# Attention and a spectral mix in one kernel: v of unit 8 in 16 small loads on SyncE's queue

## Chip, core and metric

The kernel runs on one core of a Trainium2 chip. Its time is the device time of one execution in microseconds (us); where several executions are given, their median is the number that counts. Lower is better.

## What is computed

Two layers follow each other. The first is an attention with feature maps. q, k and v have the shape (8 batches, 8 heads, 576 tokens, 64 channels). The second takes the result as x with the shape (8, 576, 512), filters 64 frequencies of each sequence with complex weights of 512 by 512, and adds a channel product with a ReLU. Everything is in float32 at the interface.

```
def phi(x):
    proj = einsum('bhsd,df->bhsf', x, w_phi)
    proj = proj - max(abs(proj), axis=-1, keepdims=True)
    return concatenate([exp(proj), exp(-proj)], axis=-1)
q_p, k_p = phi(q), phi(k)
kv = einsum('bhsf,bhsd->bhfd', k_p, v);  z = sum(k_p, axis=2)
x  = einsum('bhsf,bhfd->bhsd', q_p, kv) / (einsum('bhsf,bhf->bhs', q_p, z)[..., None] + 1e-6)
# x is laid out as (8, 576, 512)
X = rfft(x, axis=1);  Y[:, :64] = X[:, :64] @ (w_r + i*w_i)   # one 512x512 matrix per mode
u = x + irfft(Y)
out = u + maximum(u @ w_ch, 0)
```

The two weight tensors hold 64 x 512 x 512 float32 each, 64 MiB each. They are far the largest part of what has to come from memory.

## The kernel before, in words

**Units.** The attention is cut into 16 units. A unit is two batches of two heads (class `Unit`, L101); unit number n has g = n // 4 (the pair of heads) and bp = n % 4 (the pair of batches). So unit 8 is (g, bp) = (2, 0). Each unit needs three loads: `load_k` and `load_q` (L105, L109), which turn float32 into bfloat16 on the way and are 288 KB each as they land, and `load_v` (L113), which stays float32 and is 576 KB. All three go through the helper `load` (L94), which makes one DMA over 128 partitions. The v tile `vn` has two buffers (pool `pin`, L85), so v of unit n goes into the buffer that unit n - 2 has used.

**The loop.** The loop at L503 works on several units at once, in a pipeline: at step n it finishes unit n - 1 (`P`), runs the middle of unit n (`Q`), starts unit n + 1 (`K`) and turns k and q of unit n + 2 (`R`). `weigh_v2` (L182) of unit n is the one reader of its v: two VectorE multiplications `va<-vn,ee`. Right after it, at L514, the loop asks for v of unit n + 2, on GpSimd's queue (POOL). v of units 0 and 1 is asked for ahead of the loop on SyncE's queue (SP, L368 and L371). After these and the two loads of w_phi, SP has nothing to do until it stores and copies in the second half of the kernel.

**The weights.** `wload` (L340) loads an eighth of the modes for one g and one of w_r and w_i: 1 MB as it lands in bfloat16, twice that as it is read. There are 64 of them. They land in nine rotating buffers (`pw`, L83) and in some places that are free at first (`home`, L327). `next_w` (L359) issues the next one; it is called after each `mix` (L461), which multiplies the frequencies of one g by one such load. All weights, all k, q and v of the loop, and w_ch are issued by POOL, one after the other, in the order of the program (`InOrder`, L26, keeps each engine's instructions in the order in which they are written down).

**The second half.** From L574 on the last weights come in while the products with w_ch and the inverse transform are worked off. The list of those is spread over the weight loads in the loop at L923, so that TensorE has work while it waits for a weight. The last weight's `mix` comes when this list is empty. After it, the last modes are added to the outputs, and SP stores these (`store`).

**Semaphores of DMAs.** The framework gives each DMA of POOL one of eight completion semaphores in turn (the trace's landing marks carry the numbers 99 to 106 for them), and each DMA of SP one of another eight. In the trace a POOL DMA goes out only after the one eight places ahead of it has landed: the weight load of 137.26 us goes out 0.5 us after that one's landing at 136.73.

Of the kernel before, what the change touches and what calls it, by code (L numbers as in the profile page):

```python
# [21 lines left out]
NP = 4  # L22
MG = 8
NO = NMODES // MG


class InOrder:
# [16 lines left out]
def kernel(  # L44
# [15 lines left out]
    pool, sp = InOrder(tc, nc.gpsimd), InOrder(tc, nc.sync)  # L60
# [17 lines left out]
    xs = xflat[:, 16:].rearrange("p (g b n d) -> p g b n d", g=NG, b=NP, n=18)  # L78
    yacc = pers.tile([128, NO, DMODEL], F32, name="yacc")

# [13 lines left out]
    def load(t, src, g, bp, eng):  # L94
        eng.dma_start(
            t.rearrange("p b c d -> p b (c d)"),
            src[2 * bp:2 * bp + 2, 2 * g:2 * g + 2].rearrange("b h (p c) d -> (h p) b (c d)", c=9),
        )


    class Unit:  # L101
# [10 lines left out]

        def load_v(self, eng=pool):  # L113
            self.vn = pin.tile([128, 2, 9, D_], F32, name="vn")
            load(self.vn, v, self.g, self.bp, eng)

        def turn(self, src, dst, flat, part):

# [231 lines left out]
    wts = {}  # L350
    wq = [(g, mg) for g in range(2) for mg in range(2 * NO)]
    wq += [(g, mg) for g in (2, 3) for mg in range(12)]
# [29 lines left out]
    mi = scr[:, 2048:2112].bitcast(I32)  # L382
    pool.iota(mi, [[4, 2], [8, NO], [1, 4]], base=0, channel_multiplier=0)
    ident_f = scr[:, 2176:2304]
# [538 lines left out]
    while mixq:  # L923
        key = mixq.pop(0)
        g, o, i = key[0], key[1] // 2, key[1] % 2
# [128 lines left out]
```

## Time and profile before

| what | value |
|---|---|
| median of 9 runs | 440.91 us (440.36 to 442.49) |
| the profiled execution's own time | 440.36 us |
| its span, first to last instruction | 438.6 us |
| what lies outside the span | 1.8 us |
| PE busy / VectorE / ScalarE / POOL | 75% / 68% / 64% / 26% of the span |
| DMA | 99.55 MB as landed, 163.64 MB read from HBM |
| POOL's v loads (14) | 576 KB each, 24.7 us from issue to landing (median) |
| SP's v loads (units 0 and 1) | 576 KB each, 6.6 us |
| weight loads on POOL | 1024 KB each, 28.4 and 28.6 us |

A page of the profile shows one execution. `va<-vn,ee` names an instruction by the tile that it writes and those that it reads. Nearly all instructions are recorded at L37, since a helper there passes them on; so groups are told apart by tile names. "DMA wt<-in_moe_w_i_dram" is a load of weights, "vn<-in_v_dram" one of v. In a timeline the first number is the start, the second the duration, and the brackets at the end tell how long the engine had been idle before and what ended that. Beside the instructions, the trace holds a record of each DMA packet (start, duration, bytes, queue) and a mark of each DMA engine's landing: 16 marks for each DMA, one from each of the core's 16 DMA engines. The records don't tell which of the 16 engines a packet ran on.

### The profile page before, as it was taken

The page shows a single profiled execution, that of the slowest core. Times are in us where ns is not written, and L with a number is a line of the kernel's source. Part 1 is how long each engine was busy: PE and PEld are TensorE (multiplying, and loading weights), DVE is VectorE, ACT ScalarE, POOL GpSimd, SP SyncE. Part 2 cuts the span into 40 slices and gives each one's busy share as a digit, 9 for nine tenths or more (in the row PEclk, how much of TensorE's full clock was granted, in tenths as well). Part 3 has the DMA queues.
Part 4 walks back from the last instruction along what each step waited for, and adds up shares of the span by engine and source line. Part 5 has one row for each costly group of instructions (what it writes and reads, how often), then busy time and mean ns, then how long its engine had stood idle before and what let it go on. Part 6 is the DMA issues. An engine that isn't in the chain of part 4 may idle for free.

```text
span 438.6 us, 10106 instructions
## 1 busy us (share of the span) xinstructions
PE 329.3 (75%) x4190; PEld 201.0 (46%) x4233; DVE 296.0 (68%) x583; ACT 279.2 (64%) x478; POOL 112.5 (26%) x151
## 2 busy tenths in 40 slices
PE   1687677578678787787885777374679998998993
PEld 1355456456456455464554555251335454333320
DVE  5667876877785777866778878342883333885684
ACT  2786876887897676865778877310644442765782
POOL 6232132132211223222222131121101121582072
PEclk9998786999998689886889998885999999999997
DMA  8999999999999999999999999999999999997787
GB/s 192 211 210 211 234 216 237 229 220 240 236 212 238 216 232 237 237 211 238 222 226 237 211 239 212 239 212 212 212 215 223 220 221 223 212 219 155 239 364 309
DMA packets 51710, 99.55 MB, mean 227 GB/s; under 512 B 2512, under 2 KB 13648, under 8 KB 51664
## 3 DMA queue, kind: packets, MB, share of 16 engines
q0 software_dynamic: 45232, 85.86, 99.7%
q1 hardware_dynamic: 6432, 13.04, 8.6%
q8 instruction: 33, 0.54, 0.4%
q14 instruction: 13, 0.11, 0.1%
HBM read 163.64 MB, written 9.44 MB: 395 GB/s over the span
## 4 chain that ended last, share of the span: by engine, by line
DMA 34%; PE 31%; DVE 16%; ACT 12%; issue 5%; POOL 1%; POOLq 0%; ACTq 0%; DVEq 0%
PE pt L37 13%; DMA vn<-in_v_dram 11%; PE one L37 10%; DMA wt<-in_moe_w_r_dram 8%; DMA wt<-in_moe_w_i_dram 8%; ACT AB L37 6%; PE two L37 6%; DMA kb<-in_k_dram 5%; DVE mk L37 4%; DVE m L37 3%; ACT AQ L37 2%; DMA qb<-in_q_dram 2%; PE pp L37 2%; ACT XT L37 1%; DVE xw L37 1%
## 5 line engine op out<-in xcount | busy, mean ns | idle before, releaser
L37 ACT ACTIVATE AB<-two 128x1024 bf16<-128x1024 f32 x64 | 62.0, 1026 | 12.6 <-DVE mk L37 9.2
L37 ACT ACTIVATE AQ<-two 128x1024 bf16<-128x1024 f32 x64 | 62.6, 1044 | 1.8 <-PE two L37 1.5
L37 ACT CAST xw<-pt 128x512 bf16<-128x512 f32 x50 | 29.3, 587 | 41.8 <-PE pt L37 41.6
L37 DVE TENSOR_REDUCE m<-two 128x8 f32<-128x1024 f32 x32 | 39.2, 1224 | 14.1 <-PE two L37 14.0
L37 DVE TENSOR_TENSOR va<-vn,ee 128x1152 bf16<-128x1152 f32 x32 | 42.0, 1355 | 9.5 <-DMA vn<-in_v_dram 9.5
L37 DVE TENSOR_REDUCE mk<-two 128x8 f32<-128x1024 f32 x32 | 38.9, 1218 | 9.4 <-PE two L37 9.4
L37 POOL DMA_DIRECT2D wt<-in_moe_w_i_dram x28 | 20.9, 748 | 86.7 <-PE pt L37 40.4
L37 POOL DMA_DIRECT2D wt<-in_moe_w_r_dram x30 | 22.5, 750 | 70.2 <-PE one L37 31.0
L37 PE MATMUL pt<-wchb,xT 128*128 128x512 bf16 x127 | 34.3, 382 | 6.1 <-DVE xT L37 4.6
L37 ACT COPY qT<-one 128x512 bf16<-128x512 bf16 (+1 forms) x32 | 19.4, 641 | 29.9 <-PE one L37 29.5
L37 PEld LDWEIGHTS <-xs 128*128 128x128 bf16 x624 | 31.3, 102 | 13.2 <-issue 8.0
L37 PE MATMUL two<-w2blk,qT 128*128 128x256 bf16 x128 | 22.1, 301 | 19.3 <-ACT AB L37 8.3
L37 PE MATMUL one<-wt,XT 128*32 128x512 bf16 x304 | 27.1, 446 | 5.9 <-DMA wt<-in_moe_w_i_dram 4.4
L37 PEld LDWEIGHTS <-qT 128*128 128x128 bf16 x144 | 14.7, 105 | 36.8 <-issue 33.3
L37 PE MATMUL two<-mT,minus 96*128 96x512 bf16 x64 | 28.3, 443 | 3.5 <-issue 1.9
L37 PEld LDWEIGHTS <-AQ 128*128 128x128 bf16 x512 | 25.8, 111 | 8.5 <-issue 5.2
L37 PE MATMUL one<-va,AB 64*128 64x65 bf16 x1024 | 22.7, 200 | 8.9 <-DVE va L37 8.9
L37 PE MATMUL one<-kvz,AQ 128*128 128x65 bf16 x512 | 28.5, 213 | 0.8 <-ACT qT L37 0.8
L37 DVE COPY xT<-pt 128x512 bf16<-128x512 bf16 x36 | 17.0, 472 | 16.8 <-PE pt L37 16.8
L37 DVE RECIPROCAL rd<-one 128x6 f32<-128x6 f32 x48 | 9.4, 195 | 27.8 <-PE one L37 27.7
L37 DVE TENSOR_TENSOR xs<-one,rd 128x384 bf16<-128x384 f32 x48 | 26.8, 557 | 1.6
L37 PEld LDWEIGHTS <-XT 128*32 128x32 bf16 x512 | 14.6, 149 | 28.3 <-issue 21.4
(151 smaller groups left out, 713.7 us busy)
## 6 DMA issues: line engine op xcount, KB each, us to landing
wt<-in_moe_w_r_dram POOLq DMA_DIRECT2D x30, 1024.0 KB, 28.4
wt<-in_moe_w_i_dram POOLq DMA_DIRECT2D x28, 1024.0 KB, 28.6
out_dram<-of SPq DMA_DIRECT2D x16, 512.0 KB, 3.6
vn<-in_v_dram POOLq DMA_DIRECT2D x14, 576.0 KB, 24.7
kb<-in_k_dram POOLq DMA_DIRECT2D x16, 288.0 KB, 21.2
qb<-in_q_dram POOLq DMA_DIRECT2D x16, 288.0 KB, 18.6
xs<-in_moe_w_i_dram POOLq DMA_DIRECT2D x2, 1024.0 KB, 23.3
vn<-in_v_dram SPq DMA_DIRECT2D x2, 576.0 KB, 6.6
```

What stands on the lines that cost most here:

```text
L37: ins = f(*args, **kwargs)
```

## The change

v of unit 8 alone is asked for in another way. Instead of one DMA over 128 partitions on POOL's queue, `load_v` makes 16 DMAs on SP's queue, each for eight partitions (two rows of 2304 bytes in each). The call stays where it was in the program, behind `weigh_v2` of unit 6. Nothing else is changed.

```
+APART = (2, 0)
...
         def load_v(self, eng=pool):
             self.vn = pin.tile([128, 2, 9, D_], F32, name="vn")
-            load(self.vn, v, self.g, self.bp, eng)
+            if (self.g, self.bp) != APART:
+                load(self.vn, v, self.g, self.bp, eng)
+                return
+            g, bp = self.g, self.bp
+            src = v[2 * bp:2 * bp + 2, 2 * g:2 * g + 2].rearrange(
+                "b h (p c) d -> h p b (c d)", c=9)
+            for p in range(0, 128, 8):
+                sp.dma_start(self.vn[p:p + 8].rearrange("p b c d -> p b (c d)"),
+                             src[p // 64, p % 64:p % 64 + 8])
```

## The prediction

> **What bounds the kernel now.** First I read the slices and the queues of the page. A digit of 9 is a DMA share of 90% or more.
>
> ```profile
> DMA  8999999999999999999999999999999999997787
> ...
> q0 software_dynamic: 45232, 85.86, 99.7%
> q1 hardware_dynamic: 6432, 13.04, 8.6%
> q8 instruction: 33, 0.54, 0.4%
> q14 instruction: 13, 0.11, 0.1%
> ```
>
> The DMA engines are full from the second slice until the last weight is in. POOL's queue (q0) alone fills them, so what decides is not when a load is asked for but how much work each of the 16 engines has been given. Then the chain of work that ended last, in order of time:
>
> ```profile
> 266.30 36.54 DMA wt<-in_moe_w_r_dram
> 302.84 0.04 issue
> 302.88 1.63 PE pt L37 x10
> ...
> 368.76 34.47 DMA wt<-in_moe_w_i_dram
> 403.23 0.04 issue
> 403.27 0.69 PE pt L37 x8
> ```
>
> The second half begins with a weight's landing at 302.84 us, and the end hangs on the last one at 403.23; 35.4 us of the span follow. TensorE's timeline there:
>
> ```profile
> 400.77 0.38 PE L37 MATMUL pt<-xs,CF 128*128 128x512 bf16 x1
> 401.90 0.59 PE L37 MATMUL pp<-xs,CF 128*128 128x512 bf16 x2 [0.75 <-ACT xw L37]
> 403.27 0.66 PE L37 MATMUL pt<-wt,XT 128*32 128x512 bf16 x8 [0.78 <-DMA wt<-in_moe_w_i_dram]
> ```
>
> TensorE waited only 0.78 us: its own work was nearly as late as the weight. A gain counts only if both come earlier.
>
> A weight has landed when its slowest engine is done. The 16 landing marks of the last one, from the first of them, in us:
>
> ```
> 0 0.11 1.08 1.26 1.31 1.43 2.75 3.70 | 5.03 5.47 5.48 5.54 5.67 5.72 5.98 6.06
> ```
>
> Eight engines are late. Following the marks from load to load (two weight loads in a row stand 4.952 us apart on an undisturbed engine) shows why: each 16 KB refill of q8 (0.89 to 1.05 us by its packet record) puts one engine back by about 1.1 us, and through the first 17 refills, up to where my following stayed clean, they go round the same eight engines in the same order; the two groups of eight at the end fit that. The 8 KB ones of q14 (mostly 0.32 us) put three engines of the other eight back by 0.32 or somewhat more each. I call the eight heavy and light. At the landing of 302.84 the light ones reach 2.74, the heavy ones 5.81.
>
> [...]around 7.5 us v of unit 1 on SP alternates with k or q packets at 189.5 ns a pair. [...]the 33 packets of q8 are of 16,384 bytes.[...]
>
> **The change, part by part.** *Removed from POOL:* one v load. On each of 16 engines it takes 8 packets of 4608 bytes; marks stand 1.410 us apart across a v load and 4.939 instead of 4.952 across the weight behind it, so it costs 1.40 us an engine. All engines' later work comes 1.40 earlier. POOL's own issue (0.71 us) and its wait of 4.23 us ahead of it go, and the weight issued at 137.26 can go at about 132.3. That is worth nothing: eight DMAs wait in line, and the longest pause of POOL in the second half, 313.22 to 332.55, ended 11 us before the fastest engine could have run dry (it finished the load of 313.22 at 343.8).
>
> *Added on SP:* 16 issues. An issue on SP took 0.44 to 0.60 us, so they go out from 127.3 (end of `va` of unit 6) to about 137. SP has nothing else from 3 to 319 us. With eight semaphores in turn, piece 9 waits for piece 1; SP's loads took 6.6 us to land in the crowded start, so at most a few us more, with nothing behind them. VectorE's `va` of unit 8 must now wait on up to eight semaphores[...]; its v, due at 159.77, comes near 140 instead of 157.41.
>
> *The bytes on eight engines:* each gets 32 packets of 2304 bytes. Alone such packets stood 89.5 ns apart; beside POOL's 1152-byte packets (88.3 ns) the pair took 189.5, so 101. That is 2.86 to 3.24 us, and 16 marks of 9 to 22 ns add 0.14 to 0.35: 3.0 to 3.6, I take 3.3. A pause for each piece to start isn't shown: the small refills put an engine back by no more than they took (0.32), the large ones by about 0.16 more; at 0.16 a piece the cost would be 6.2. That is the upper end; below 3.0 nothing is known to go. Net: +1.9 us on eight engines, -1.40 on the other eight.
>
> *What it collides with:* SP's packets overtake the loads in line from 127 to 137 us, v of unit 7 among them, and VectorE already waits for that one. The second such wait, of unit 15, comes later:
>
> ```profile
> 124.67 2.62 DVE L37 TENSOR_TENSOR va<-vn,ee 128x1152 bf16<-128x1152 f32 x2
> ...
> 143.14 1.36 DVE L37 TENSOR_TENSOR va<-vn,ee 128x1152 bf16<-128x1152 f32 x1 [2.16 <-DMA vn<-in_v_dram]
> ...
> 283.10 1.36 DVE L37 TENSOR_TENSOR va<-vn,ee 128x1152 bf16<-128x1152 f32 x1 [7.38 <-DMA vn<-in_v_dram]
> ```
>
> On the light engines that v lands by 141.7 now, so with 3.3 more at 145.0: 1.9 us later (on the heavy ones 3.3). The units behind it slip by as much, until the wait of 7.38 us at 283.10 swallows it. If that cover were gone, 1.9 us would reach the end.
>
> **The sum, on the profiled 440.36.** Light eight: the last weight's marks become 3.70 + 1.9 = 5.60 at most there, and 6.06 - 1.40 = 4.66 on the heavy ones. Landing 6.06 - 5.60 = 0.46 us earlier. The landing of 302.84 comes 5.81 - max(2.74 + 1.9, 4.41) = 1.17 earlier, so TensorE's own work is ready about 1.2 earlier and doesn't hold it up. 440.36 - 0.46 = 439.90. The profiled run is 0.55 under the median, so 440.91 - 0.46 = 440.45 as a median. A cost of 3.0 gives -0.76, one of 3.6 gives -0.16; from 3.76 nothing is left.
>
> **The rivals.** *Heavy eight, or some of each.* If the eight engines that SP uses carry refills of PE, the slowest one gets 1.9 on top of 6.06, all 100 us of the second half shift, and the end is 1.9 later: 442.8. With half of them heavy it is 1.6 to 1.9. It decides from one heavy engine among the eight with a mark above 4.2. For it: nothing in the records names an engine. Against it: the light eight are just those that PE's refills leave out, including the three with the small refills, [...]and I lean to light. *The pieces cost more.* Light eight, but a pause for each piece: 0.16 each makes the marks 3.70 + 4.8 = 8.5, 2.4 later: 443.3. Against it: the small refills pay none. *The change doesn't do what it says:* pieces spread evenly over 16 engines. Each gets 1.65 for 1.40: +0.25, 441.2.[...]
>
> **How the numbers follow.** Light eight at the cost taken 0.52 (own range 440.0 to 441.0), heavy or mixed 0.34, dear pieces 0.06, even spread 0.08. The time is that of the first. The range reaches from 439.8 (cost 3.0 and a little noise) to 443.1 (heavy or mixed, with its noise); 443.3 and more is left out. About 0.2%, 0.9 us, is what a measurement of this kernel can tell from no change. Faster by more: only from the light eight with a cost under 2.9, 0.18. Slower by more: heavy, mixed and dear, 0.38. Between: 0.44.
>
> **What would show it.** Right: the weight landing at 302.84 comes about 1.2 us earlier, the last one 0.3 to 0.8 earlier, the spread of its marks falls from 6.06 to about 5.6 with the order of groups nearly closed; v of unit 7 lands near 145 and `va` waits about 4 us for it, while the wait for v of unit 15 shrinks to about 4.5; q1 grows by 0.59 MB. Wrong: the last weight's spread grows to 9 or more (heavy), or all marks shift alike (even spread), or the wait for v of unit 15 is gone and slips reach the second half.

## The result: slower

| | median | range | runs |
|---|---|---|---|
| before | 440.95 us | 439.88 to 442.71 | 33 |
| after | 442.85 us | 441.60 to 444.44 | 10 |

The ratio is 1.0042, with a 95% interval of 1.0030 to 1.0054. The forecast was 440.45; the time of the rival "heavy eight, or some of each" was 442.8. The profiled execution of after took 443.97 us (span 442.2), 1.1 us more than its median.

First the slices and the queues of after's page, to be held against those of before.

```profile
DMA  8999999999999999999999999999999999996688
...
q0 software_dynamic: 45088, 85.27, 98.9%
q1 hardware_dynamic: 6816, 13.63, 8.9%
q8 instruction: 33, 0.54, 0.4%
q14 instruction: 13, 0.11, 0.1%
```

0.59 MB have moved from q0 to q1. The instruction refills (q8 and q14) are as they were, and the engines are as full as before. The prediction took q8 for TensorE's: in before's trace 172 to 397 TensorE instructions, weight loads counted, start between one packet of q8 and the next, and 6 to 76 of VectorE's. That fits, but no record names the engine. Now after's chain of waits at the three places that the prediction named (start, duration, what was waited for):

```profile
114.13 32.05 DMA vn<-in_v_dram
...
268.55 35.53 DMA wt<-in_moe_w_r_dram
...
370.09 35.44 DMA wt<-in_moe_w_i_dram
```

Start and duration add up to the landing. v of unit 7 lands at 146.18 (near 145 was forecast), and VectorE waits for it:

```profile
146.20 2.63 DVE L38 TENSOR_TENSOR va<-vn,ee 128x1152 bf16<-128x1152 f32 x2 [2.93 <-DMA vn<-in_v_dram]
```

The weight of 302.84 lands at 304.08, 1.24 us later, where 1.17 earlier was forecast. The last weight lands at 405.53 instead of 403.23, 2.30 later. TensorE meets it with the same small wait as before:

```profile
405.57 0.66 PE L38 MATMUL pt<-wt,XT 128*32 128x512 bf16 x8 [0.76 <-DMA wt<-in_moe_w_i_dram]
```

So in this pair of profiles the loss came in through the DMA engines: 2.30 us of it were there when the last weight landed, against 1.9 between the medians. What is more than that in the profiled time (3.6 us against before's) lies behind the landing, where the granted clock (the third figure from the end of the row) was 0.82 in this execution:

```profile
405.60:415.00 9.40, 8.71 (x44) 4.13 (x45) 4.36 (x8) 4.41 (x9) 0.00 (x0) 0.82 0.42 115
```

In a second profile of the same kernel, told of below, the stretch behind the landing ran at 1.00, so I take this part for chance:

```profile
404.90:414.30 9.40, 8.82 (x52) 3.84 (x52) 5.62 (x9) 5.17 (x10) 0.00 (x0) 1.00 0.56 150
```

The 16 landing marks of the last weight, from the first of them (396.93), in us:

```
0 1.36 | 3.94 4.21 4.28 4.37 5.62 5.73 5.99 6.01 6.03 6.09 6.39 | 8.34 8.47 8.60
```

Before, six marks lay within 1.5 us of the first. Now two do: the only engines that carry neither large refills nor pieces. Three come 2 us behind all others. I followed each engine's marks from load to load once more. While the pieces moved, eight engines stepped on through the weights without being put back; six of these are engines that the large refills go round, two are not. So SP's eight are the rest: **six light engines and two heavy ones**, and the two heavy ones have the last marks, 8.47 and 8.60. The third late mark, 8.34, is by the same following a light engine of SP's eight: none of the large refills put it back, but small ones of q14 did. On its own it would have let the weight land at 405.27, 2.04 us later than before. So in this execution eight light engines would not have been faster either.

Yet the size doesn't fit. The mean of the 16 marks should have moved by 1.65 - 1.40 = +0.25 us (3.3 us on eight engines is 1.65 on each of 16). It moved by +1.45 (mean over the 16 marks of the weight that landed at 193.14 before; about the same on all later loads). So the pieces cost not 1.65 us an engine but 2.85 (1.45 + 1.40). Something besides the bytes took DMA time.

### The profile page after: what moved, and what is told of

Same layout as the page of the kernel before. It is cut to its first block, busy times and chain, and to the rows that moved or that the text cites. A ratio compares the mean times of both kernels' runs of the same rounds, so it can differ in the third digit from the quotient of the medians.

```text
span 442.2 us, 10138 instructions
## 1 busy us (share of the span) xinstructions
PE 330.8 (75%) x4190; PEld 202.0 (46%) x4233; DVE 296.0 (67%) x583; ACT 279.4 (63%) x478; POOL 111.7 (25%) x150
## 4 chain that ended last, share of the span: by engine, by line
DMA 34%; PE 29%; DVE 15%; ACT 14%; issue 5%; POOL 1%; POOLq 0%; ACTq 0%; DVEq 0%
PE pt L38 13%; DMA vn<-in_v_dram 11%; PE one L38 9%; DMA wt<-in_moe_w_r_dram 8%; DMA wt<-in_moe_w_i_dram 8%; ACT AB L38 6%; PE two L38 5%; DMA kb<-in_k_dram 5%; DVE mk L38 4%; DVE m L38 4%; ACT AQ L38 3%; DMA qb<-in_q_dram 2%; PE pp L38 2%; ACT XT L38 2%; DVE xw L38 1%
## 5 line engine op out<-in xcount | busy, mean ns | idle before, releaser
L38 POOL DMA_DIRECT2D kb<-in_k_dram x16 | 11.5, 718 | 64.2 <-PE one L38 56.0
```

The costliest lines, as they stand in the source:

```text
L38: ins = f(*args, **kwargs)
```

## Experiments

**Theory.** (1) Two of the eight engines that SP uses carry refills, so they set the end. (2) The extra cost comes from where the pieces write: as the change cuts them, the eight engines of a piece write eight neighbouring partitions at once. This was the author's guess; the two profiles don't show it. **Rivals.** The small DMAs cost something as such, wherever they write. Or eight engines reading one stretch of memory get into each other's way. Or v of unit 7 comes late, and the delay reaches the end through the units.

"Mean cost" below is the shift of the mean mark at the weight of 193.14, plus the 1.40 taken off; each version has one profile, and a second profile of before shifts it by 0.23, one of the change by 0.61. So a difference below some 0.6 between two versions says little.

### All 16 engines, or 16 neighbours

One DMA over 128 partitions on SP (`e1_whole`):

```
-            for p in range(0, 128, 8):
-                sp.dma_start(self.vn[p:p + 8]..., src[p // 64, p % 64:p % 64 + 8])
+            load(self.vn, v, g, bp, sp)
```

> v of unit 8 on SyncE's queue as one DMA over 128 partitions, which all 16 engines share. Theory 'mixed eight' (the 16 pieces fall on eight engines, two of which also carry TensorE's refills and set the end): every engine trades 1.40 us for about 1.65, so the last weight's spread stays near 6.1 us, its landing moves by 0.2 to 0.9, and the time is 441.0 to 441.8. Rival 'delay through the units' (v of unit 7 comes 3 us later, the units slip, and that reaches the end): v of unit 7 is overtaken all the same, so the time is 442.5 to 443.

Measured: 441.08 us, ratio 0.9992 (0.9978 to 1.0006); mean cost 1.56 us, spread of the last marks 6.25, v of unit 7 lands at 144.67. The even spread that the prediction had as a rival to the change costs nothing that can be measured, though v of unit 7 is 1.55 us late. The wait for the last weight, against 0.78 before:

```profile
404.05 0.67 PE L38 MATMUL pt<-wt,XT 128*32 128x512 bf16 x8 [1.14 <-DMA wt<-in_moe_w_i_dram]
```

A delay of v of unit 7 of this size doesn't reach the end by itself.

The same in 8 pieces of 16 partitions (`e2_p16`):

```
-            for p in range(0, 128, 8):
+            for p in range(0, 128, 16):
```

> The same v in 8 pieces of 16 partitions[...]. 'Mixed eight': as with one DMA, 441.0 to 441.8, spread near 6.1 us. Rival 'small pieces as such' (each small DMA costs its engines a start, whichever engines they are): [...]about half of the extra over one DMA returns on all engines, and the last weight lands 1 us or more after that of the one-DMA version, with an unchanged spread: 442.0 to 442.5.

Measured: 442.14 us, ratio 1.0020 (1.0008 to 1.0032), mean cost 2.64, spread 6.44. The spread is near that of `e1_whole`, as with equal shares on all engines, yet the loss (1.11 us between the medians) is more than half of the change's. It sits in the packets: those of SP took 106 ns in the first two pieces and 162 on average over all, against 107 with one DMA. v of unit 7 lands at 146.54, later than with the change, and still less is lost: **the delay through the units is out** as the main cause. This run doesn't tell small pieces from writes to neighbours; the next ones do.

### Where the pieces write, and where they read

Three versions keep 16 pieces of eight partitions. In the first the partitions of a piece stand 16 apart, in the second 4 apart. The third writes neighbours as the change does, but reads rows that stand 16 apart.

```
 # e4_strided
+            for p in range(16):
+                sp.dma_start(self.vn[p::16]..., src[p::16])
 # e7_ports
+            for p in [32 * a + j for a in range(4) for j in range(4)]:
+                sp.dma_start(self.vn[p:p + 29:4]..., src[p:p + 29:4])
 # e8_src
+            for i in range(16):
+                sp.dma_start(self.vn[8 * i:8 * i + 8]..., src[i::16])
```

> 16 pieces of eight partitions as in the change, at the same time, but the partitions of a piece stand 16 apart, so that its eight engines don't write into the same neighbouring partitions. If the collision is one of eight engines at one place of SBUF, the packets fall back from 144 to 154 ns to about 106 and the extra 1.2 us on all engines goes: last weight 1 us earlier than with the change, 441.7 to 442.0, spread still 8 to 9. If the place is nothing to it: as the change, 442.9. 'Delay through the units' expects 442.9 too.

> 16 pieces of eight partitions as in the change, but the partitions of a piece stand 4 apart[...]. [...]SyncE's packets stay at 106 ns throughout, v of unit 7's fall back towards the undisturbed 178 ns (314 with the change, 218 to 243 with 16 apart), the first mark of the last weight comes 1.2 to 1.5 earlier than before the change, the last one still 1.5 to 2.2 later (two of SyncE's eight engines carry TensorE's refills), time 441.3 to 442.3.[...]

> The counterpart: a piece writes eight neighbouring partitions as in the change, but reads rows of v that stand 16 rows apart in memory, as in the version with 16 apart (so v of unit 8 lies in other partitions than its k; this part of the result is another one, the work is the same). [...]as the change, v of unit 7's packets at 300 ns or more beside the pieces, mean mark of the last weight 1.3 to 1.6 later than before, 442.6 to 443.2. Rival 'the place in memory' (eight engines read one 18 KB stretch of memory at once): as with 16 apart, mean mark 0.7 later, 441.5.

| version | median, us | ratio (95%) | mean cost, us | SP's 256 packets, sum, us | v of unit 7, ns a packet |
|---|---|---|---|---|---|
| e7, 4 apart | 441.63 | 1.0014 (1.0002 to 1.0025) | 1.77 | 27.1 | 200 |
| e4, 16 apart | 441.50 | 1.0006 (0.9990 to 1.0022) | 2.09 | 27.6 | 222 |
| the change, neighbours | 442.85 | 1.0042 (1.0030 to 1.0054) | 2.85 | 31.9 | 304 |
| e8, reads apart, writes neighbours | 442.48 | 1.0035 (1.0014 to 1.0056) | 3.09 | 35.0 | 349 |

(Undisturbed, v of unit 7's packets take 180 to 184 ns; the last column counts those beside SP's pieces.) The versions that write eight neighbours a piece cost more than the others and have the longer medians, whatever is read; all four have 16 small pieces of eight partitions. 4 apart and 16 apart can't be told from each other by the cost or the medians; v of unit 7's packets, 222 and 200 ns, do differ. So neither the pieces as such nor the place in memory is the cause of the large extra cost. What in the writing of neighbours holds the packets back, no run shows. The version with 16 neighbours (2.64) is nearer to the change (2.85, in a second profile 2.24) and e8 (3.09), the single DMA (1.56) to 4 apart and 16 apart (1.77, 2.09). The rows of busy times by stretch show it without counting packets. Here is 139 to 143 us, in which v of unit 7 moves, for before, the version 4 apart, the change, and e8; the last two figures are the share of busy DMA engines and GB/s.

```profile
139.00:143.00 4.00, 3.16 (x49) 2.14 (x46) 1.64 (x3) 3.93 (x5) 0.70 (x1) 1.00 1.09 272
```

```profile
139.00:143.00 4.00, 3.16 (x53) 2.26 (x52) 2.13 (x4) 3.24 (x5) 0.00 (x0) 1.00 1.12 286
```

```profile
139.00:143.00 4.00, 3.73 (x73) 3.00 (x70) 2.62 (x5) 2.83 (x5) 0.00 (x0) 1.00 1.11 231
```

```profile
139.00:143.00 4.00, 3.22 (x60) 2.49 (x60) 2.13 (x4) 3.24 (x5) 0.00 (x0) 1.00 1.16 208
```

The engines are as busy in all four (1.09 to 1.16); with pieces of eight neighbours they move 231 and 208 GB/s, with partitions 4 apart 286. The busy share doesn't show the loss, since a slowed packet counts for as long as it lasts.

The version 4 apart also bears on step (1), since its packets cost about what the prediction reckoned (1.77 against 1.65). By the prediction's sum, light engines alone would have made it faster than before; it is slower by 0.57 us (0.1 to 1.1). Its last marks, from 396.34:

```
0 0.60 | 3.30 3.34 3.64 4.12 5.18 5.20 5.29 5.35 5.55 5.58 5.73 | 8.00 8.16 8.74
```

Two early, three far behind, as in after. By the same following two of the three are heavy, 8.74 among them, and one, 8.00 or 8.16, is again the light engine with small refills. Without the heavy two the weight would have landed at 404.3 to 404.5: later than in before's first profile (403.23), earlier than in its second (404.74, below). So the run shows that the heavy two are there; that they alone make it slower than before, it doesn't show.

### Later

SP waits for `va` of unit 7 first, by way of a small DMA that reads it.

```
+    after_va = pm.tile([1, 16], BF16, name="after_va", bufs=1)
...
+            sp.dma_start(after_va, va[0:1, 1, 0, 0:16])
```

> The same 16 pieces, but SyncE first waits for va of unit 7, so that they run at about 146 to 158 us, when no other v is moving. 'Mixed eight' with a collision (the extra cost of some 1.2 us on the other eight engines, and 0.5 on SyncE's eight, comes from v of unit 7 being written at the same time): the first mark of the last weight comes 1.2 to 1.5 us earlier than before the change instead of 0.2 earlier, the last one 1.5 to 2.0 later, so the spread grows to about 9; time 442.3 to 442.8. Rival 'small pieces as such': marks as with the change, first 0.2 earlier, last 2.3 later, 442.9.

Measured: 444.29 us, ratio 1.0056 (1.0033 to 1.0080): a miss for both. No v was moving at 150 to 163 us, but SP's packets took 131 ns in the first 5 us and 200 in the rest, 44.5 us in sum: beside weights, k and q, whose packets stretched too in the later part (weights from 173 to 182 ns, k and q from 107 to 128). My reading that a full-rate v must be there for the collision is wrong. Why the change's own first pieces stayed at 106 ns beside weights, I can't say. This time v of unit 8 was itself late:

```profile
164.73 2.63 DVE L38 TENSOR_TENSOR va<-vn,ee 128x1152 bf16<-128x1152 f32 x2 [4.58 <-DMA vn<-in_v_dram]
```

so the run has two causes in it and sizes neither.

### Which engines

The pieces are cut into sizes from one partition to eight, to load the engines unequally (`e9_ladder`).

```
+            for j, m in enumerate(4 * (7, 6, 5) + (4, 4, 4, 8)):
+                for a, b in ((j, j + 16 * m - 15), (j + 16 * m, j + 113)):
+                    if a < b:
+                        sp.dma_start(self.vn[a:b:16]..., src[a:b:16])
```

> v of unit 8 in pieces of 7+1, 6+2, 5+3, 4+4 and 8 partitions, 16 apart[...]. Its use is to name the engines: the order in which the marks are put back gives each engine's number, and with TensorE's refills the number of each engine that carries them. Theory 'mixed eight':[...] the last landing comes 4 to 5 us later than before and the time is 445 to 446;[...] light engines decide and it is 441.5 to 443.[...]

Measured: 441.51 us, ratio 1.0013 (1.0006 to 1.0020). The marks fit two heavy engines among the eight, but what each engine got came out ambiguous, several orders fitting equally well. The last weight landed at 404.69, 1.46 later than in before's first profile and not 4 to 5, the forecast for a heavy engine with much of the load. So no heavy engine got as much as that; which engines are light, and what share each got, the run doesn't tell.

Then a quarter of v of unit 8 went in pieces of three partitions and one of two, and the rest on POOL (`e10_light`). That a piece of three falls on three engines was the author's estimate, from the eight landing marks of each piece of eight in after; it was not shown for these pieces.

```
+            pool.dma_start(self.vn[32:128]..., (v of the unit)[32:128])
+            for a, b in [(j, j + 21) for j in range(10)] + [(30, 32)]:
+                s = 10 if b - a > 2 else 1
+                sp.dma_start(self.vn[a:b:s]..., src[a:b:s])
```

> Only a quarter of v of unit 8 (partitions 0 to 31) goes on SyncE's queue, in ten pieces of three partitions 10 apart and one of two[...]; the other 96 partitions stay on GpSimd's queue, which takes 0.35 us off every engine. The three engines get some 2.3 us each. If they carry none of TensorE's large refills[...], the light ones end at 3.70 + 2.3 - 0.35 = 5.65 at most, the heavy ones at 5.71: the last weight lands 0.35 earlier and the time is 440.5 to 441.0, not to be told from no change. If one of them carries refills, the last mark comes 1.9 later: 442 to 443, and the spread of the last marks reaches 8.

Measured: 440.76 us beside 441.34 for before on the same chip, ratio **0.9985 (0.9974 to 0.9995)**: faster than both kernels, by little. The spread of the last marks was 6.47. TensorE no longer waits for the last weight at all:

```profile
403.15 0.59 PE L38 MATMUL pp<-xs,CF 128*128 128x512 bf16 x2 [0.75 <-ACT xw L38]
403.67 0.66 PE L38 MATMUL pt<-wt,XT 128*32 128x512 bf16 x8
```

With a heavy engine among those of the pieces the spread was expected to reach 8. So these engines are light, or each got less than was reckoned. The gain is one comparison, 0.2 to 1.1 us by its interval, and the sum doesn't explain its size. The 0.35 us off every engine didn't come: POOL's 96 packets took 225 ns on average, where the 128 of a whole v take 179 to 184, so each engine was spared only some 0.1 us. Why the time fell by more stays open.

The same for unit 12 as well (`e14_light2`; "240 us less" in its text is a slip and means nothing).

```
-APART = (2, 0)
+APART = ((2, 0), (3, 0))
```

> As the version with three engines, for v of unit 12 too: [...]All engines get another 0.35 us off, the three another 2.3 us. If those three still have room (the first time took 0.58 us off the median, more than the 0.35 reckoned): 240 us less is not in question, 440.2 to 440.6 where the kernel before has 441.1. If one of them is at the limit, its mark becomes the last one and the gain is gone: 441 to 442.3, with one to three marks 1 us or more behind the heavy ones.

Measured: 440.80 us, ratio 1.0001 (0.9989 to 1.0013). The gain is gone. Three reasons fit and weren't separated: the first gain may have been in part chance, the engines of the small pieces may have reached the limit (seven of the marks now lie within 1 us of the last), and POOL's loads of 96 partitions spare little time: their packets took 241 and 230 ns on average (units 8 and 12), against 179 to 184 for a whole v.

### Twice the dose

v of units 8 and 12 in 16 pieces each (`e5_two`), with the same edit to `APART`.

> v of unit 12 as well as that of unit 8 in 16 pieces. [...]the cost adds up, SyncE's eight engines are put back by another 2.2 us and the other eight by nothing or little, so the last weight's spread goes from 8.6 to about 11 and the time to 444.5 to 445.5. Rival 'delay through the units': the second delay comes where TensorE waits anyway and adds under 0.5 us: 443 to 443.4.

Measured: 445.93 us, ratio 1.0110 (1.0095 to 1.0125); spread 11.83. The second v costs about 3 us, more than the first, though its packets piled up less (106 to 122 ns). One reading is that the first v had to use up a margin, and that what is put on the engines that are last reaches the end in full. No run tests it, and by the reckoned 1.9 a v it would explain 2 us of the 3.

### Both kernels once more

> The kernel before once more, for how far one profile differs from the next: its first profile was 0.6 us under the median and most others stood 0.1 to 2 us above theirs. Expected: last weight at 403.2 to 404.5, spread of its marks 5.5 to 6.5, eight late marks, 440.4 to 442.0. If the last weight lands near 404.3, a landing 2.3 later in the changed kernel's profile and a median 1.9 later are the same finding, and the other versions' landings have to be read against 404.3 too.

> The changed kernel once more, beside the version with three engines on the same chip: 442.5 to 443.2. Last weight at 404.8 to 405.8, two or three marks 2 us or more behind all others, whichever engines the round of refills reaches first; the mean cost of the pieces over 16 engines 2.7 to 3.1 us.

Before: 441.88 us, last weight at 404.74, marks up to 7.28 (the next one 6.18). After: 443.01 beside 441.34, ratio 1.0035 (1.0021 to 1.0049), last weight at 404.84, mean cost 2.24; the pieces went out 4.2 us earlier than in its first profile and only their end met v of unit 7, but the stretch shows a loss of speed too (242 GB/s, where before's two profiles have 272 and 274):

```profile
139.00:143.00 4.00, 2.02 (x16) 0.88 (x15) 0.00 (x0) 4.00 (x6) 0.70 (x1) 1.00 1.11 242
```

TensorE's wait for the last weight in before's second profile:

```profile
404.78 0.66 PE L37 MATMUL pt<-wt,XT 128*32 128x512 bf16 x8 [0.94 <-DMA wt<-in_moe_w_i_dram]
```

In after's second profile:

```profile
404.88 0.66 PE L38 MATMUL pt<-wt,XT 128*32 128x512 bf16 x8 [0.78 <-DMA wt<-in_moe_w_i_dram]
```

The landing of the last weight moves by 1.5 us from one execution of before to the next, mostly by its one slowest engine. After's second profile is of the fastest of its 18 executions (441.46 us), its first of one 1.1 us above the median. So a single pair of profiles sizes nothing below that: the 2.30 of the first pair is 0.10 in the second. The medians, 1.9 and 1.7 us, are what counts. In this second profile of after too, the last three marks are the two heavy engines and the light one with small refills, at 6.96 to 7.16 from the first.

## Why the prediction was wrong

- **What bounds the kernel**: right. The engines are full (90% or more in every slice of after's page from 11 to 398 us), and the slowest engine's mark of the last weight sets the end (405.53 in after, where TensorE goes on at 405.57). A second load on the same engines made it slower (`e5_two`); a smaller one, in pieces of three partitions, made it a little faster in one comparison (`e10_light`).
- **Eight pieces' engines**: all pieces did fall on the same eight engines. For the prediction this was an estimate that before's trace didn't show, since each of its DMAs leaves 16 marks. After's trace bears it out with eight landing marks for each of the 16 pieces (behind one mark that comes 0.4 to 0.8 us after the issue: for the first eight pieces from 130.04 to 132.77 us, before any of the data, which start at 132.92), and with the two early marks that are left.
- **"I lean to light"**: this step failed. It was a guess from the sizes of two groups. SP's eight are six light engines and two heavy ones. The working for that case stood among the rivals, 1.6 to 1.9 us. In the version where the extra cost is nearly gone (4 apart, `e7_ports`), it is 0.57 (0.1 to 1.1). I put the difference down to before's profile: its slowest mark was 6.06, in the second one 7.28, and against the latter the two heavy engines have 1.2 us less to lose. That is argued from two profiles, not shown.
- **"3.70 + 1.9 = 5.60 at most" on the light engines**: this term failed as well, and in after it would have been enough to turn the sign. On the same scale the slowest light engine of SP's eight came to 8.10 in after (405.27) and to 7.2 or 7.3 in `e7_ports`, where the price is nearly as reckoned. So light engines have less room than before's marks say. Small refills put that engine back too; how much of the rest they explain stays open.
- **The price of the pieces, 3.3 us on eight engines (1.65 on each of 16)**: mis-sized. The term nearly holds when the partitions of a piece stand 4 apart (1.77). With eight neighbours it was 2.85 and 2.24. The price was taken from SP's packets beside POOL's in the first microseconds, where both loads covered 128 partitions; that eight engines would now write eight neighbours didn't enter. (The 1.40 us that the removed load gives back stand: across ten v loads and the weights behind them the median steps of the marks are 1.48 and 4.86, not 1.410 and 4.939, but their sum agrees within 0.01.) By the medians this is the larger part: some 1.1 to 1.3 of the 1.7 to 1.9 us. The rival "dear pieces" had the right place, but the pause for each start that it reckoned with doesn't show: 16 pieces 4 apart cost 1.77 for the 1.65 reckoned without one.
- **v of unit 7 near 145, `va` waits about 4 us**: 146.18 and 2.93 us. **The wait for v of unit 15 shrinks to about 4.5**: it stayed, at 7.16 us, because the weights and that v came later themselves (284.38 instead of 283.08). So the slip of the units was swallowed, as reckoned:

```profile
284.40 2.63 DVE L38 TENSOR_TENSOR va<-vn,ee 128x1152 bf16<-128x1152 f32 x2 [7.16 <-DMA vn<-in_v_dram]
```

- **SP's issues**: 9.63 us from 129.58 on, where 127 to 137 was forecast, piece 9 behind piece 1 as reckoned (its first mark is at 135.05, piece 1's last one at 134.57), and nothing behind them:

```profile
129.58 9.63 SPq L38 DMA_DIRECT2D vn<-in_v_dram  x16
```

- **The chances**: "heavy or mixed" had 0.34 and is what SP's eight are. That its 442.8 is so near the measured 442.85 is luck: its working has the heavy engines alone, and leaves out where the pieces write. The range, 439.8 to 443.1, held the time, since it reached to that case.

## What to carry to other kernels

With the DMA engines full, a load had no single price here: 16 pieces on eight engines cost more or less by what else these engines carried and by where the pieces wrote. Ask how many landing marks a shape leaves, what else its engines carry, and how close together the partitions of a piece stand. Cut small loads so that the partitions of a piece stand apart (4 or 16 here), or leave them whole; pieces of eight neighbours cost a quarter to three quarters more DMA time than those 4 apart (2.24 to 3.09 us against 1.77). And before a gain of 1 us is worked out from the marks of one profile, see a second one: the slowest engine's mark moved by more than that.

## What the runs showed of the hardware that was not expected

- SP's pieces of eight neighbours and POOL's v load slowed each other: 2304-byte packets went from 106 to 189 ns, each a mean of 16 in a row (the change), 4608-byte packets from 180 to 304 (the change) and 349 ns (e8), with the engines' busy share from 139 to 143 us nearly unchanged (1.09 to 1.16).
- The eight engines that the 16 KB instruction refills go round (0.89 to 1.11 us a packet, 33 of them) are neither SP's eight nor the other eight. Each of the 16 pieces left eight landing marks; by the marks from load to load, two of SP's eight carry such refills, and six of the other eight do.
- A DMA over 96 partitions on POOL took 225 to 241 ns a packet on average, one over 128 179 to 184: fewer bytes, but not in proportion less time.
